# One batch of a sparse-attention and hard-swish kernel goes by four heads with both halves of their queries, and its loads stand between the weights

## The chip, the cores and the metric

One core of one Trainium2 chip. The metric is device time in microseconds (us). Engines are named as the profile names them: PE (TensorE's matmuls; PEld its weight loads), DVE (VectorE), ACT (ScalarE), POOL (GpSimd), SP (SyncE, which here only issues transfers); PEq, SPq and so on are their sequencers.

## What is computed

Attention over 4 batches of 8 heads, 768 positions, 64 features. Each query keeps the 6 chunks of 32 keys with the largest upper bound on its score. The result, laid out as 3072 tokens by 512 features, goes through two dense layers with a hard-swish between them.

```python
ub = np.sum(np.maximum(q[:, :, :, None, :] * k_min[:, :, None, :, :], q[:, :, :, None, :] * k_max[:, :, None, :, :]), axis=-1)
ub = np.where(causal, ub, -1000000000.0)
top_chunks = np.argsort(ub, axis=-1)[..., -top_k:]
scores = scale * np.matmul(q, k.transpose(0, 1, 3, 2))
mask = sel & (pos[:, None] >= pos[None, :])
...
h = x @ w_in
relu6 = np.clip(h + 3.0, 0.0, 6.0)
g = h * relu6 / 6.0
return (g @ w_out).astype(np.float32)
```

## The kernel before

Heads go in 16 pairs; batch b has pairs 4b to 4b+3. Two pairs are a quad (four heads, loaded together). The 768 queries of a head go in two halves of 384. A **unit** is one quad with one half, so a batch has four units, 16 in all. Names of tiles, which are also the names in the rows:

- A unit is prepared (`prepare`): K and Q come from memory (`KS`, `QS`), are transposed (`KF`, `QF`; on DVE for batches 1 to 3), K's chunks give maximum and minimum (`KMA`, DVE's reduces, `limits`), and POOL or ACT casts them to the score operands (`KL`, `QLA`); `QR` is the rectified query.
- `bounds` computes the upper bounds on PE into `UBT`. From batch 1 on, the units are taken two at a time, each on its own corners of the array. In half 0 of batches 1 to 3 only the later 192 queries need full precision: `coarse` units do the first 192 in bf16 (the "guard" matmuls, with `QLA`) and the rest in fp32.
- `attend` picks the chunks on DVE (`UB`, `T`, `SELA`, `MT`), copies the mask beside the query operand (`masks_out`), and then for each pair does the score tiles on PE (`SPS`, two buffers), the exponentials on ACT (`PT`), the causal triangle on POOL, and the product with the values on PE (`PVP`, from `VB`, which POOL casts from `VT`). DVE scales the product into `Xb`. A pair has two score tiles in half 0 (1024 and 512 columns) and four in half 1 (1024, 1024, 768, 1024).
- When the four pairs of a half of a batch are done, its 384 tokens are a group: they are transposed into `XT` (by PE in batch 0, by a transposing transfer from batch 1 on), 16 `hidden` steps of four matmuls give `HP`, ACT or DVE and then DVE turn it into `GT`, and `result` steps of four matmuls each add up `OP` with `WOUT`; ACT or DVE scales that into `OT`, and SP stores it. `WIN` and `WOUT` are each loaded in two halves from POOL's queue, with a cast to bf16. A small copy of a loaded element (`seenWIN`, `seenWOUT`) makes POOL wait for an earlier load before it issues one. The first half of `WOUT` serves result parts 0 and 1, the second half parts 2 and 3.

What stands where is decided by hand-kept tables. `SEQ` gives the order of the first loads (K, Q or V with the number of the unit whose quad is loaded; I and O for halves of `WIN` and `WOUT`); SP has at most three transfers of later batches under way (`ring=3`). `FIRST_TO_LAST` gives the order of all steps on each engine, by step number; every engine then runs its list strictly in that order, waiting where an operand is not there. `LANDED` and the lengths in `add(...)` only feed the program that hands out buffers in that order. PE starts with up to 16 matmuls on zeros (`busy`, line 343 after the change) that do no work of the reference.

Of the kernel before, what the change touches and what calls it, by code (L numbers as in the profile page):

```python
# [135 lines left out]
def kernel(  # L136
# [101 lines left out]

    units = []
    for b in range(B):  # L240
        for half in range(2):
            for n in range(2):
                first = (2 * b + n) * 2
                units.append((pairs[first:first + 2], half))
# [158 lines left out]
    def coarse(b, half):  # L403

        return b > 0 and half == 0
# [11 lines left out]
    def bounds(us):  # L417
# [3 lines left out]
        rough = coarse(us[0]["two"][0]["b"], us[0]["half"])  # L421
        for part, which in ([("guard", 1), ("guard", 0)] if rough else []) + [("all", 1), ("all", 0)]:
            for u in us:
                for i, st in enumerate(u["two"]):
# [242 lines left out]
    SEQ = "K0 Q0 K1 Q1 Q2 K2 V0 V1 Q3 K3 V3 I0 V2 I1 O0 O1 K4 Q4 K5 Q5 V4 V5"  # L667
# [5 lines left out]
    add = plan.add  # L673
# [12 lines left out]
    def arrive(engine, issue, length, run, after=(), take=(), parts=1, ring=False):  # L686
# [3 lines left out]
        for part in range(parts):  # L690
# [5 lines left out]
            if at:  # L696
                behind = [w for w in weights[-1:]] if engine == "POOL" else []
                landed.append(add("WIRE", at, 0, after=[got] + behind, give=lane, least=1.5 if engine == "SP" else 5.6 if behind else 8.8))
                if engine == "POOL":
                    weights.append(landed[-1])  # L700
            else:
                landed.append(add("DMA", length, 0, after=[got], give=lane))
        return landed

    LANDED = dict(SP=[7.05, 7.65, 8.27, 8.87, 9.46, 10.07, 10.67, 11.26, 11.87, 12.47, 13.08, 13.68, 14.28, 14.88, 15.48, 16.08, 16.70, 18.50, 18.95, 19.60, 20.05, 20.45, 20.85, 21.30, 22.30, 22.70, 23.25, 23.80, 26.05, 26.40, 27.30, 41.60, 50.30, 51.40, 52.90, 54.20, 55.70, 57.20, 58.60, 60.00, 61.40, 62.80, 64.10, 64.80, 67.20, 68.80, 69.50, 70.40, 71.40, 72.20, 73.00, 73.70],
                  POOL=[32.30, 37.90, 43.30, 50.10])
# [77 lines left out]
    def prepare(n):  # L784
# [64 lines left out]
        if us:  # L849
# [3 lines left out]
            a = add("PE", 1.25 if len(us) == 1 else 0.8 if coarse(two[0]["b"], half) else 1.27, r + RANK["sel"] + BOUND[n], later(bounds, us), tile=2, after=sum([u["chain"] for u in us], []),  # L853
# [88 lines left out]
    for n_group, ((b, half), xs) in enumerate(finished.items()):  # L942
# [16 lines left out]
        if (b, half) in CROSS:  # L959
            lane = hold("lane")  # L960
            got = add("SP", 1.25, -3000, later(cross_tokens, g), after=xs, take=[held_xt, lane])
            xt.append(add("DMA", 2.0, 0, after=[got], give=[x, x, lane]))
# [11 lines left out]
        for t in range(HB):  # L974
# [21 lines left out]
        PE="""  # L996
# [14 lines left out]
            1574 1569 1575 1576 1570 1577 1581 1585""",  # L1011
        ACT="""
# [81 lines left out]
```

## Time and profile before

| | |
|---|---|
| three timed runs | 265.73 us median (265.18 to 266.31) |
| the profiled execution | 266.49 us |
| its span, first to last instruction | 264.8 us |
| busy PE / DVE / ACT / POOL | 255.5 / 207.7 / 187.2 / 121.6 us |
| moved by transfers | 32.15 MB, mean 121 GB/s |

The span is 1.7 us shorter than the execution's own time, and that execution is 0.76 us above the median of the timed runs. A busy share is an average over stages; matmuls overlap, and their ends are modelled, so a PE that is busy for a whole stretch can still have lost time in it.

### The profile page before, as it was taken

The numbers are of one execution on the slowest core, as the hardware profiler recorded it, in microseconds if no ns is written. First come the engines' busy times: TensorE is split into PE (matmuls) and PEld (weight loads), VectorE is DVE, ScalarE is ACT, GpSimd is POOL, SyncE is SP. The second block draws the span as 40 slices with busy tenths as digits, with TensorE's granted clock in tenths as the row PEclk, the third lists the DMA queues.
The fourth block names the chain that finished last, engine by engine and source line by source line (L and its number), as shares of the span: only waits on it lengthen the run. The fifth ranks groups of instructions, "written<-read, shape, count | busy, mean of one in ns | idle before, by whom it ended". The sixth has DMA issues, their size and how long they took to land.

```text
span 264.8 us, 6528 instructions
## 1 busy us (share of the span) xinstructions
PE 255.5 (96%) x2399; PEld 150.6 (57%) x2424; DVE 207.7 (78%) x577; ACT 187.2 (71%) x308; POOL 121.6 (46%) x282
## 2 busy tenths in 40 slices
PE   6999999999999989999999999999999999999995
PEld 3557566645454666654656575654666666555443
DVE  7889789899897998899877869997986266979001
ACT  3889879667668899847888988855897683634121
POOL 8332834246459775184777382485287221000000
PEclk9999999999999999999999999999999999999999
DMA  8999999999945989997998299832100421301023
GB/s 162 217 201 176 202 202 217 170 128 172 214 97 128 168 158 172 132 146 181 127 132 109 45 185 171 171 62 79 42 1 0 63 79 42 59 4 40 0 82 119
DMA packets 128528, 32.15 MB, mean 121 GB/s; under 512 B 122224, under 2 KB 124528, under 8 KB 128496
## 3 DMA queue, kind: packets, MB, share of 16 engines
q1 hardware_dynamic: 123760, 27.14, 62.9%
q0 software_dynamic: 3136, 4.19, 9.3%
q10 hardware_dynamic: 1600, 0.39, 0.7%
q8 instruction: 19, 0.31, 0.5%
q14 instruction: 13, 0.11, 0.2%
HBM read 27.26 MB, written 6.29 MB: 127 GB/s over the span
## 4 chain that ended last, share of the span: by engine, by line
PE 79%; ACT 6%; DMA 5%; DVE 4%; SPq 2%; issue 2%; ACTq 0%; DVEq 0%
PE OP L631 27%; PE HP L613 27%; PE SPS L517 10%; PE PVP L551 7%; DMA QS<-in_q_dram 5%; ACT PT L529 4%; PE UBT L435 4%; DVE GT L624 2%; PE OP L640 1%; PE SPS L498 1%; SPq L203 1%; ACT U L621 1%; PE SPS L501 1%; DVE QF L359 1%; SPq L195 1%
## 5 line engine op out<-in xcount | busy, mean ns | idle before, releaser
L529 ACT ACTIVATE PT<-SPS 128x1024 bf16<-128x1024 f32 (+2 forms) x96 | 84.8, 915 | 17.3 <-PE SPS L517 12.7
L613 PE MATMUL HP<-XT,WIN 128*128 128x384 bf16 x512 | 91.5, 326 | 0.7 <-DVE GT L624 0.6
L631 PE MATMUL OP<-WOUT,GT 128*128 128x512 bf16 x343 | 85.1, 379 | 1.4 <-issue 0.2
L624 DVE SCALAR_TENSOR_TENSOR GT<-U,HP 128x384 bf16<-128x384 bf16 x128 | 66.2, 544 | 15.0 <-ACT U L621 13.0
L621 ACT ACTIVATE U<-HP,THREE 128x384 bf16<-128x384 f32 x98 | 55.4, 580 | 22.4 <-PE HP L613 19.6
L613 PEld LDWEIGHTS <-WIN 128*128 128x128 bf16 x512 | 48.7, 98 | 33.7 <-issue 1.9
L631 PEld LDWEIGHTS <-GT 128*128 128x128 bf16 x368 | 34.8, 98 | 35.4 <-issue 1.2
L534 POOL TENSOR_SCALAR_AFFINE_SELECT PT<-PT 128x256 bf16<-128x256 bf16 x84 | 33.8, 412 | 38.1 <-ACT PT L529 37.3
L517 PE MATMUL SPS<-QLA,KL 128*128 128x384 bf16 (+2 forms) x240 | 37.8, 278 | 0.9 <-ACT PT L529 0.9
L517 PEld LDWEIGHTS <-KL 128*128 128x128 bf16 x240 | 22.0, 98 | 17.0 <-issue 2.5
L309 POOL TENSOR_SCALAR_AFFINE_SELECT QLA<-QF 64x384 bf16<-64x384 f32 (+1 forms) x43 | 21.4, 502 | 14.3 <-DVE QF L359 11.1
L551 PEld LDWEIGHTS <-PT 128*128 128x128 bf16 x672 | 24.0, 97 | 4.0 <-issue 1.6
L551 PE MATMUL PVP<-VB,PT 128*128 128x65 bf16 x672 | 26.0, 193 | 0.2
L309 POOL TENSOR_SCALAR_AFFINE_SELECT KL<-KF 64x384 bf16<-64x384 f32 x33 | 16.4, 501 | 12.2 <-DVE KF L359 11.2
L619 DVE TENSOR_SCALAR U<-HP 128x384 bf16<-128x384 f32 x30 | 16.5, 551 | 4.5 <-PE HP L613 4.2
L657 ACT ACTIVATE OT<-OP 128x512 f32<-128x512 f32 x15 | 8.9, 592 | 14.5 <-PE OP L631 13.8
L567 DVE TENSOR_TENSOR Xb<-PVP,RINV 128x384 bf16<-128x384 f32 x32 | 17.8, 557 | 1.1
L223 POOL TENSOR_SCALAR_AFFINE_SELECT QLA<-MT 64x768 bf16<-64x768 bf16 x13 | 11.0, 846 | 13.2 <-DVE MT L470 6.9
L359 DVE STREAM_TRANSPOSE KF<-KS 128x384 f32<-128x384 f32 x24 | 13.2, 562 | 1.5 <-DMA KS<-in_k_dram 1.0
L392 ACT ACTIVATE QR<-QF 128x192 bf16<-128x192 f32 (+2 forms) x36 | 12.9, 407 | 1.8 <-DVE QF L359 1.6
L359 DVE STREAM_TRANSPOSE QF<-QS 128x384 f32<-128x384 f32 x24 | 12.5, 548 | 1.9 <-DMA QS<-in_q_dram 1.5
L374 DVE TENSOR_REDUCE KMA<-KF 128x12 f32<-128x384 f32 x24 | 12.9, 539 | 0.2
(89 smaller groups left out, 267.7 us busy)
## 6 DMA issues: line engine op xcount, KB each, us to landing
out_dram<-OT SPq DMA_DIRECT2D x23, 256.0 KB, 2.3
KS<-in_k_dram SPq DMA_DIRECT2D x24, 192.0 KB, 5.2
QS<-in_q_dram SPq DMA_DIRECT2D x24, 192.0 KB, 5.7
VT<-in_v_dram SPq DMA_DIRECT2D x24, 192.0 KB, 4.4
WIN<-in_moe_w_in_dram POOLq DMA_DIRECT2D x2, 1024.0 KB, 9.9
WOUT<-in_moe_w_out_dram POOLq DMA_DIRECT2D x2, 1024.0 KB, 15.2
VS<-in_v_dram SPq DMA_DIRECT2D x12, 128.0 KB, 3.9
KS<-in_k_dram SPq DMA_DIRECT2D x9, 128.0 KB, 3.9
```

What stands on the lines that cost most here:

```text
L309: nc.gpsimd.affine_select(out=to, in_=x, pattern=[[0, n]], compare_op=A.is_ge, fill=0.0, base=0, channel_multiplier=0)
L359: nc.vector.transpose(T[:], st[name][:, st["i"], half * HC:(half + 1) * HC, :].rearrange("p c e -> p (c e)"))
L517: nc.tensor.matmul(SP[:, j, c0:c0 + n], lhsT=KLS[st["pair"] % 6][:, j, jb * P:(jb + 1) * P], rhs=st["QL", half][:, j, at:at + n], start=Tr ...
L529: nc.scalar.activation(PT[:, :, 0:cols], SP[:, :, 0:cols], ACT.Exp, scale=scale)
L534: nc.gpsimd.affine_select(out=PT[:, :, c0:c0 + P], in_=PT[:, :, c0:c0 + P], pattern=[[0, 2], [1, P]], compare_op=A.is_ge, fill=0.0, base=0 ...
L551: nc.tensor.matmul(PVP[:, j, n, :], lhsT=PT[:, j, c0:c0 + P], rhs=st["VB"][:, jb, j, :], start=(jb == 0), stop=(jb == qb))
L567: nc.vector.tensor_tensor(out=to, in0=PVP[:, :, :, 0:D], in1=RINV[:].to_broadcast([P, 2, HB, D]), op=A.mult)
L613: nc.tensor.matmul(HP[:], lhsT=WIN[:, kt, f * P:(f + 1) * P], rhs=g["XT"][:, :, kt, :] if (g["b"], g["half"]) in CROSS else g["XT"][:, kt, ...
L619: nc.vector.tensor_scalar(U[:], g["HP", f][:], 3.0, 0.0, op0=A.add, op1=A.max)
L621: nc.scalar.activation(U[:], g["HP", f][:], ACT.Relu, bias=THREE[:], scale=1.0)
L624: nc.vector.scalar_tensor_tensor(out=g["GT"][:, f, :], in0=g["U", f][:], scalar=6.0, in1=g["HP", f][:], op0=A.min, op1=A.mult)
L631: nc.tensor.matmul(g["OP", t][:], lhsT=g["GT"][:, f, t * P:(t + 1) * P], rhs=WOUT[:, f, :], start=(f == 0), stop=(f == FT - 1))
```

## The change

Units 4 to 7 (batch 1) are numbered anew: before, they were quad 0 half 0, quad 1 half 0, quad 0 half 1, quad 1 half 1; now quad 0 half 0, quad 0 half 1, quad 1 half 0, quad 1 half 1. So the two units that `bounds` takes together are now a coarse and a full one, and the order of its parts goes per unit. In `SEQ` the loads of batch 1's first quad (K4 Q4 V4) stand between the halves of `WIN` and those of `WOUT`, and those of its second quad (now K6 Q6 V6) behind `WOUT`. All five lists of `FIRST_TO_LAST` are new (their numbers are left out here).

```diff
+    BY_QUADS = [1]
     units = []
     for b in range(B):
-        for half in range(2):
-            for n in range(2):
-                first = (2 * b + n) * 2
-                units.append((pairs[first:first + 2], half))
+        for i in range(4):
+            n, half = (i // 2, i % 2) if b in BY_QUADS else (i % 2, i // 2)
+            first = (2 * b + n) * 2
+            units.append((pairs[first:first + 2], half))
...
-        rough = coarse(us[0]["two"][0]["b"], us[0]["half"])
-        for part, which in ([("guard", 1), ("guard", 0)] if rough else []) + [("all", 1), ("all", 0)]:
+        for part, which in (("guard", 1), ("guard", 0), ("all", 1), ("all", 0)):
             for u in us:
+                rough = coarse(u["two"][0]["b"], u["half"])
+                if part == "guard" and not rough:
+                    continue
...
-    SEQ = "K0 Q0 K1 Q1 Q2 K2 V0 V1 Q3 K3 V3 I0 V2 I1 O0 O1 K4 Q4 K5 Q5 V4 V5"
+    SEQ = "K0 Q0 K1 Q1 Q2 K2 V0 V1 Q3 K3 V3 I0 V2 I1 K4 Q4 V4 O0 O1 K6 Q6 V6"
...
-                landed.append(add("WIRE", at, 0, after=[got] + behind, give=lane, least=1.5 if engine == "SP" else 5.6 if behind else 8.8))
+                landed.append(add("WIRE", at, 0, after=[got] + behind, give=lane, least=1.5 if engine == "SP" else 5.6 if behind else 7.9))
...
-                  POOL=[32.30, 37.90, 43.30, 50.10])
+                  POOL=[32.20, 38.40, 57.50, 63.20])
...
     FIRST_TO_LAST = dict(
         PE="""
-            0 1 2 3 4 5 6 148 156 149 157 7 8 9 10 11 12 165 173 164 166 13 174 231 223 14 181 188 230 222 15 190 195 197 238 193 208 248
+            0 1 2 3 4 148 156 149 157 5 6 7 173 165 164 166 174 8 9 10 223 231 11 12 13 14 15 222 181 230 188 190 195 238 197 208 240 193
...
```

How the change moves instructions, at three places. First POOL's queue where `WOUT` is loaded; before, right behind the second half of `WIN`, with the small copy waiting for a V load (`VS`) of batch 0:

```order
L290 COPY seenWIN_634<-VS 1x1
L293 DMA WIN<-in_moe_w_in_dram 128x4x1024
L378 TENSOR_TENSOR KMA<-KMA 128x12 x2
L290 COPY seenWOUT_663<-VS 1x1
L296 DMA WOUT<-in_moe_w_out_dram 128x8x512
```

The same after the change, from the last work ahead of `WOUT` to the casts of V behind its second half:

```order
L291 COPY seenWOUT_1100<-QS 1x1
L297 DMA WOUT<-in_moe_w_out_dram 128x8x512
L310 AFFINE_SELECT KL_107<-KF 64x384
L223 AFFINE_SELECT KL_101<-EB 64x768
L310 AFFINE_SELECT KL_107<-KF 64x384
L310 AFFINE_SELECT QLA<-QF 64x384 x2
L291 COPY seenWOUT_1177<-QS 1x1
L297 DMA WOUT<-in_moe_w_out_dram 128x8x512
```

The load of `WOUT` now waits for the last Q transfer of batch 1's first quad, and four casts of that quad stand between its halves. Second, PE at batch 1's first two `UBT` groups; before, the end of the coarse group and, later, the whole of the full one:

```order
L435 LDWEIGHTS KMA
L435 MATMUL UBT<-QR,KMA 32x192
L435 MATMUL UBT<-QF,KMA 32x192 x8
L435 MATMUL UBT<-QR,KMA 32x192 x8
L631 LDWEIGHTS GT
...
L435 MATMUL UBT<-QF,KMA 32x384 x8
L435 MATMUL UBT<-QR,KMA 32x384 x8
```

After the change, the end of the first group; the second one reads the same:

```order
L438 LDWEIGHTS KMA
L438 MATMUL UBT<-QR,KMA 32x192
L438 MATMUL UBT<-QF,KMA 32x192 x4
L438 MATMUL UBT<-QF,KMA 32x384 x4
L438 MATMUL UBT<-QR,KMA 32x192 x4
L438 MATMUL UBT<-QR,KMA 32x384 x4
L634 LDWEIGHTS GT
```

A group of eight 192-column matmuls and one of eight 384-column ones have become two of four and four. Third, ACT's list from the last exponentials of half 0 in batch 1 (before) to the first `U` of its first group of tokens:

```order
L529 ACTIVATE PT<-SPS 128x2x256
L529 ACTIVATE PT<-SPS 128x1024 x2
L529 ACTIVATE PT<-SPS 128x2x384
L529 ACTIVATE PT<-SPS 128x1024 x3
L529 ACTIVATE PT<-SPS 128x2x384
L529 ACTIVATE PT<-SPS 128x1024 x3
L305 CAST KL_106<-KF 64x384
L529 ACTIVATE PT<-SPS 128x2x384
L529 ACTIVATE PT<-SPS 128x1024
L621 ACTIVATE U<-HP,THREE 128x384 x2
```

The same after the change, for the second quad (pairs 6 and 7), whose half 0 and half 1 now stand together, up to the same `U`:

```order
L532 ACTIVATE PT<-SPS 128x1024
L532 ACTIVATE PT<-SPS 128x2x256
L660 ACTIVATE OT<-OP 128x512
L532 ACTIVATE PT<-SPS 128x1024
L532 ACTIVATE PT<-SPS 128x2x256
L532 ACTIVATE PT<-SPS 128x1024 x2
L532 ACTIVATE PT<-SPS 128x2x384
L532 ACTIVATE PT<-SPS 128x1024 x3
L532 ACTIVATE PT<-SPS 128x2x384
L532 ACTIVATE PT<-SPS 128x1024
L624 ACTIVATE U<-HP,THREE 128x384 x9
```

The exponentials of the first quad (pairs 4 and 5), with casts and copies between them, now stand ahead of these.

## Rows read from the trace of the kernel before

**Rows 1.** The page's line of busy time: us, share of the span, instructions.

```profile
PE 255.5 (96%) x2399; PEld 150.6 (57%) x2424; DVE 207.7 (78%) x577; ACT 187.2 (71%) x308; POOL 121.6 (46%) x282
```

**Rows 2.** Stretches: us, busy PE, PEld, DVE, ACT, POOL (instructions), granted clock, transfers, GB/s.

```profile
90.00:100.00 10.00, 9.10 (x127) 6.41 (x127) 9.61 (x25) 9.66 (x13) 6.23 (x16) 1.00 1.01 178
120.00:260.00 140.00, 138.94 (x1214) 81.69 (x1230) 101.82 (x280) 93.05 (x149) 55.93 (x125) 1.00 0.46 80
```

**Rows 3.** What PE waited for: us in total, times, longest.

```profile
PE SPS L517 <- ACT PT L529: 0.9, 3, 0.4
PE HP L613 <- DVE GT L624: 0.6, 1, 0.6
```

**Rows 4.** Timeline of PE, then DVE, at batch 1's first bounds: start, us, instruction.

```profile
71.77 0.26 PE L435 MATMUL UBT<-QLA,KMA 64*32 64x192 bf16 x4
72.33 0.51 PE L435 MATMUL UBT<-QLA,KMA 64*32 64x192 bf16 x4 [0.29 <-DVE GT L624]
...
73.62 1.67 PE L631 MATMUL OP<-WOUT,GT 128*128 128x512 bf16 x6
...
70.24 1.04 DVE L359 STREAM_TRANSPOSE QF<-QS 128x384 f32<-128x384 f32 x2 [1.28 <-DMA QS<-in_q_dram]
```

**Rows 5.** The chain that ended last: start, us, what (a transfer: issue to landing).

```profile
17.71 1.42 PE UBT L435 x16
...
63.96 6.16 DMA QS<-in_q_dram
...
81.78 1.45 PE UBT L435 x32
...
120.48 0.94 PE UBT L435 x48
...
161.88 6.50 PE HP L613 x40
```

**Rows 6.** Timeline of PE at batch 1's scores: one of three tiles that waited.

```profile
95.91 0.61 PE L517 MATMUL SPS<-QLA,KL 128*128 128x384 bf16 x4 [0.39 <-ACT PT L529]
```

**Rows 7.** The chain in a narrower stretch: a score tile and a values product that waited for nothing.

```profile
88.68 0.44 PE SPS L517 x4
...
93.69 0.92 PE PVP L551 x30
```

**Rows 8.** ACT's exponentials by form: count, busy us, mean ns, idle before.

```profile
L529 ACT ACTIVATE PT<-SPS 128x1024 bf16<-128x1024 f32 x64 | 63.9, 1022 | 11.2 <-PE SPS L517 8.0 <-PE SPS L501 1.5 <-PE SPS L505 1.1
...
L529 ACT ACTIVATE PT<-SPS 128x768 bf16<-128x768 f32 x16 | 12.9, 807 | 4.2 <-PE SPS L517 3.1 <-PE SPS L501 0.9
...
L529 ACT ACTIVATE PT<-SPS 128x512 bf16<-128x512 f32 x16 | 9.6, 599 | 1.9 <-PE SPS L517 1.7
```

**Rows 9.** Transfers: SP's issues (start, us), then `WIN` and `WOUT` by line (ns; starts).

```profile
22.40 19.67 SPq L203 DMA_DIRECT2D KS<-in_k_dram  x4
...
54.31 5.28 SPq L203 DMA_DIRECT2D KS<-in_k_dram  x4
...
L293 POOL DMA_DIRECT2D WIN<-in_moe_w_in_dram x2: 768/880/991, 23.7 to 27.3; - x2
...
DMA to landing us min/median/max: 8.5/9.9/11.4
...
L296 POOL DMA_DIRECT2D WOUT<-in_moe_w_out_dram x2: 891/910/930, 28.5 to 35.5; - x2
...
DMA to landing us min/median/max: 14.9/15.2/15.5
```

**Rows 10.** Timeline of PE at its first results, and at its start.

```profile
49.45 1.02 PE L631 MATMUL OP<-WOUT,GT 128*128 128x512 bf16 x3
...
1.06 3.17 PE L342 MATMUL SPS<-ZERO 128*128 128x512 bf16 x7 [1.06 <-DVE ZERO L251]
...
7.01 1.46 PE L342 MATMUL SPS<-ZERO 128*128 128x512 bf16 x6
```

**Rows 11.** The tile `XT`: its transposing transfers.

```profile
DMA to landing us min/median/max: 3.6/3.8/4.1
```

More of the change, by code (lines that the diff above doesn't have):

```diff
@@ L703, in arrive @@
         return landed
-    LANDED = dict(SP=[7.05, 7.65, 8.27, 8.87, 9.46, 10.07, 10.67, 11.26, 11.87, 12.47, 13.08, 13.68, 14.28, 14.88, 15.48, 16.08, 16.70, 18.50, 18.95, 19.60, 20.05, 20.45, 20.85, 21.30, 22.30, 22.70, 23.25, 23.80, 26.05, 26.40, 27.30, 41.60, 50.30, 51.40, 52.90, 54.20, 55.70, 57.20, 58.60, 60.00, 61.40, 62.80, 64.10, 64.80, 67.20, 68.80, 69.50, 70.40, 71.40, 72.20, 73.00, 73.70],
-                  POOL=[32.30, 37.90, 43.30, 50.10])
+    LANDED = dict(SP=[7.05, 7.65, 8.27, 8.87, 9.46, 10.07, 10.67, 11.26, 11.87, 12.47, 13.08, 13.68, 14.28, 14.88, 15.48, 16.08, 16.70, 18.00, 19.00, 19.60, 20.05, 20.45, 20.85, 21.30, 22.30, 22.80, 23.35, 23.90, 26.00, 26.40, 27.20, 40.00, 41.40, 42.80, 44.20, 45.60, 47.00, 48.40, 49.30, 50.10, 51.00, 51.80, 63.50, 64.90, 66.30, 67.70, 69.10, 70.50, 71.90, 73.30, 74.20, 75.00, 75.90, 76.70],
+                  POOL=[32.20, 38.40, 57.50, 63.20])
     FIRST = dict(KS=(3.65, 4.63), QS=(5.6, 6.43))
@@ L852, in prepare @@
             held = [hold("m") for u in us]
-            a = add("PE", 1.25 if len(us) == 1 else 0.8 if coarse(two[0]["b"], half) else 1.27, r + RANK["sel"] + BOUND[n], later(bounds, us), tile=2, after=sum([u["chain"] for u in us], []),
+            a = add("PE", 1.25 if len(us) == 1 else 0.8 if coarse(two[0]["b"], half) else 1.37 if two[0]["b"] in BY_QUADS else 1.27, r + RANK["sel"] + BOUND[n], later(bounds, us), tile=2, after=sum([u["chain"] for u in us], []),
                     take=held, give=used)
@@ L960 @@
             lane = hold("lane")
-            got = add("SP", 1.25, -3000, later(cross_tokens, g), after=xs, take=[held_xt, lane])
-            xt.append(add("DMA", 2.0, 0, after=[got], give=[x, x, lane]))
+            got = add("SP", 1.42, -3000, later(cross_tokens, g), after=xs, take=[held_xt, lane])
+            xt.append(add("DMA", 1.6, 0, after=[got], give=[x, x, lane]))
         for a in range(0, 0 if (b, half) in WORDS + CROSS else KT_HID, 2):
@@ L996 @@
         PE="""
[14 rows of a table removed]
-            1574 1569 1575 1576 1570 1577 1581 1585""",
-        ACT="""
[10 rows of a table removed]
-            1553 1556 1562 1514 1565 1507 1571 1582 1586""",
-        DVE="""
[13 rows of a table removed]
-            1559 1563 1560 1566 1578""",
-        POOL="""
[8 rows of a table removed]
-            1000 1007 1010 1013""",
-        SP="""
[4 rows of a table removed]
-            1508 1572 1579 1583 1587""",
[14 rows of a table added]
+            1575 1569 1576 1570 1577 1581 1585""",
+        ACT="""
[10 rows of a table added]
+            1494 1523 1526 1529 1535 1538 1541 1544 1547 1550 1556 1559 1562 1507 1500 1565 1514 1571 1582 1586""",
+        DVE="""
[12 rows of a table added]
+            1483 1486 1489 1492 1521 1495 1524 1527 1530 1532 1533 1536 1539 1542 1545 1548 1551 1553 1554 1557 1560 1563 1566 1578""",
+        POOL="""
[7 rows of a table added]
+            878 891 877 953 892 921 881 955 948 899 895 956 896 906 909 988 989 905 961 964 967 974 980 977 997 994 1000 1007 1010 1013""",
+        SP="""
[4 rows of a table added]
+            1572 1579 1583 1587""",
     )
```

94 rows, old and new, of tables (ACT, DVE, PE, POOL) are left out of this document.

## The prediction

> **What bounds the kernel now.** I read the busy line first: PE is busy 255.5 of 264.8 us, and no other engine is over 78% [rows 1]. The stretches say where PE still loses time: from 120 to 260 us it is busy 138.9 of 140, and nothing can be won there, while from 90 to 100 us it is busy 9.1 of 10, with ACT and DVE at 9.7 and 9.6 [rows 2]. So the change can win at most the few waits that PE has ahead of 120 us. The list of PE's waits [rows 3] and the timeline name them, and the reader is to see three. At batch 1's first bounds DVE stands 1.28 us for the last Q transfer, and the `UBT` group behind it takes from 71.77 to 73.62 us, 1.85 us, where the same group at 120.48 takes 0.94 [rows 4, 5]. At batch 1's scores three tiles wait for an exponential to free one of the two score buffers, 0.9 us together, and each then shows 0.60 where an unhindered one shows 0.44 [rows 3, 6, 7]. Once PE waits 0.6 us for a `GT` [rows 3]. All three lie where the order and the loads are new.
>
> **The change, part by part.** The number of score, value, hidden and result matmuls stays. What moves is when they stand, and one group of matmuls changes its form.
>
> *The late Q transfer.* The first bounds of batch 1 now need only the first quad, whose loads stand ahead of `WOUT`. The second half of `WIN` lands at 27.3 + 11.4 = 38.7 us [rows 9]. Then some 6.5 of the quad's eight K and Q transfers are left, at 5.28/4 = 1.32 us each [rows 9]: 47.3 us. PE comes to these bounds at about 63 us (below). POOL's casts for them are queued behind copies that wait for the first half of `WOUT`, at 56 us by the next part, with some eleven instructions, at 0.5 each (an estimate, as DVE's): 61.5. So the wait goes: 1.85 - 0.94 = **-0.9**. The second quad's Q land some seven transfers behind `WOUT`, 62.8 + 9.2 = 72.0; DVE then has about eleven instructions of 0.5 us [rows 4], so the second bounds can begin at some 78, and PE reaches them at 80. That is covered by 2 us; later by more, and it costs PE us for us.
>
> *The exponentials.* Before, from the end of pair 4's last tile to the start of pair 6's last one PE has seven score tiles (five of 0.44 and two of 0.33), one short and two long value products (12 and 30 matmuls, 0.37 and 0.92): 5.1 us, the shorter tiles and products in proportion to the rows [rows 7]. ACT has six exponentials of 1.02 and one of 0.81: 6.9 [rows 8]. The difference is 1.8, the trace shows 0.9 + 3 x 0.16 = 1.35, so ACT's pace is about 0.07 shorter than the means. After, the first quad's exponentials stand between result steps, and the narrow place is the second quad: from the end of pair 6's first tile to the start of pair 7's last one PE has ten score tiles (3.7), three short and three long value products (3.9) and three result steps (2.6): 10.2 us. ACT has seven of 0.95, one of 0.74, two of 0.53 and one scaling of `OT` (0.6, as an exponential of its 512 columns): 9.0. ACT keeps up with 1.2 us to spare: **-1.35**.
>
> *The wait for GT.* It stands behind DVE's reduces. They now stand two at a time between the `GT` instructions. I take **-0.4** (0, if it comes back, to -0.6).
>
> *The bounds in their new form.* Before, two coarse units together take 0.94 and two full ones 1.45, 2.39 in all [rows 5]. After there are two mixed groups. From below: a mixed group holds a full unit, so it is not under 1.42; with 1.45 each it is +0.5. From above: nothing overlaps, 1.42 + 0.94 each, 4.7 in all, +2.3. The nearest row is that a full unit alone takes 1.42 and two take 1.45: the second rides along. The coarse unit's fp32 matmuls then ride along too, and only its guard matmuls have no partner: 0.94 less half of 1.45 is 0.2. So 1.65 each: **+0.9**.
>
> *WOUT later.* PE's first result begins at 49.45 [rows 10]. After, 60 more hidden matmuls stand ahead of it, at 6.50/40 = 0.163 us [rows 5], and a group of 12 transposes (0.7, an estimate by their columns): 59.9. The second half of `WOUT` is asked for eight results and four hidden matmuls on, at 62.3. POOL issues the first half when the quad's last Q lands, 47.3; a first half took 8.5 us with other loads beside it, and the next ones landed 5.3 and 6.4 us apart (38.7, 28.5 + 15.5 = 44.0, 35.5 + 14.9 = 50.4) [rows 9]. That is 56.0, and 61.3 to 62.4 for the second. The quad's four V transfers run beside it, which can cost up to 2.6 us more (an estimate: half of a K transfer each, since K's pieces are half as long). I take 62.9: **+0.6** (0 to 2.5). PE stands idle in that time, and behind the first result on PE stand the hidden steps that feed DVE and ACT.
>
> Here a rule speaks against the change. The rows: while the weights moved, SP needed 19.67 us to get four K transfers out, and 5.28 without them [rows 9]; the weights kept their 5.3 to 6.4 us. So it is the K transfers that yield. The Trainium skill, "DMA: Bandwidth & Descriptors", section "Queues, rings and completion order", says that each transfer engine goes round-robin between the queues it has work for. The trace agrees only in that both move; the turns are not of equal worth here. With turns of equal worth the three K transfers under way would hold up `WOUT` by their whole length, which is the slower rival below.
>
> *Tokens of batch 1's half 0.* They are complete only after pair 7, and from that product to the first hidden step PE has 5.1 us (six score tiles, two long products, one result step). The transfer takes 3.6 to 4.1 [rows 11], which leaves 1.0 for DVE's two scaling instructions. **+0.2** (0 to 0.7, one more DVE instruction ahead).
>
> *Start and stores.* PE now has five fillers ahead of the first transposes instead of seven; it waits for K and Q there anyway: 0 (-0.3 to +1.1, a rival). Stores move on SP, but nothing waits for them.
>
> Sum: -0.9 - 1.35 - 0.4 + 0.9 + 0.6 + 0.2 = -0.95. The profiled execution took 266.49, so 265.5; it stands 0.76 above the median of the runs, 265.73, so on that scale **264.8 us**.
>
> **Rivals.**
>
> *All covers hold.* `WOUT` and the tokens come in time, and the mixed bounds cost their least: -0.9 - 1.35 - 0.6 + 0.5 = -2.35, so 263.4. For it: 2 to 6 us of margin on the first quad. Against: every new cover is an estimate from a transfer's pace.
>
> *WOUT is held up (slower).* Place: the third result part on PE, at 62.3. The K transfers of the second quad are in the queue beside `WOUT`; if two of the three go ahead in full, 2 x 1.32 later, the second half lands at 65.6 and PE waits 3.3 instead of 0.6: 267.5. It decides from a landing of about 65.2 on, where the time is 0.5% above before. For it: SP's queue will have three transfers ready the moment V is in. Against: how the weights kept their pace before.
>
> *The exponentials are only crowded elsewhere, so the change does not do what it says.* The second quad has both halves at one place. If two result steps of PE fall out of that place by a wait of ACT's casts or mask copies, ACT is 0.5 us short of PE, and with the hand-overs the old 1.35 comes back: 266.1. Against: the 1.2 us to spare.
>
> *The clock at the start.* Seven matmuls of 512 columns take 3.17 us at the start, six take 1.46 from 7.01 [rows 10]: the first run at the lower of the two levels, 1.2 GHz, the later at 2.4, though the granted clock reads 1.00 throughout. Before the rise PE was at work without a gap. With five fillers there is a gap ahead of the first transposes. If the clock rises only some us later, the first bounds (1.42 at the higher level [rows 5]) take 1.4 longer, part of it under the wait for Q: +1.1, 265.9. The Trainium skill, "TensorE: Matmul & The Clock Gate", section "What's actually happening", says that the default state is throttled and that activity releases it; by that, less activity ahead can mean a later rise, and the trace of before cannot show it.
>
> **How the numbers follow.** Forecast 264.8, by its own terms 264.0 to 265.6: 0.46. All covers hold, 263.4: 0.24. `WOUT` held up, 267.5: 0.15. Exponentials crowded, 266.1: 0.08. Clock, 265.9: 0.07. 0.5% of 265.73 is 1.33 us, about what a measurement of this kernel can tell from no change: faster is under 264.4, slower over 267.06. Faster: nearly all of the second case and a third of the first, 0.40. Slower: most of the third, 0.14. The same: 0.46. The range reaches from the best case's lower side to the bound where the slower rival decides: 262.9 to 267.1.
>
> **What would show it.** Right: the first `UBT` group of batch 1 runs at about 63 us without a wait for Q; both take 1.5 to 1.8 us; no score tile of batch 1 waits for an exponential; the first result begins near 60, with a wait under 1 us for `WOUT` two parts on; from 120 us on the trace reads as before. Wrong: a wait of over 2 us of PE at the first results; a wait of DVE for K or Q of the first quad, behind which `GT` stands and so PE's hidden steps; the first hidden step of batch 1 waiting for `XT`; a start in which the transposes of the first Q keep the lower clock.

## The result, and the profile after

The changed kernel takes 268.74 us (median of six runs, 266.80 to 270.39) beside 265.60 for the kernel before: ratio 1.0122, 95% interval 1.0091 to 1.0154. The forecast was 264.8. The profiled execution took 269.50 (span 267.8), and it stands 0.76 above its median, as the one of before did. Medians here and below are over all runs of a kernel; ratios leave out the runs in which the chip showed its slower state.

PE's part of the line of busy time has grown little (before: [rows 1]); the list of PE's waits says where the rest went. The page's line, then the waits (us in total, times, longest):

```profile
PE 257.2 (96%) x2402; PEld 151.6 (57%) x2424; DVE 204.3 (76%) x571; ACT 194.1 (73%) x320; POOL 119.5 (45%) x276
```

```profile
PE OP L634 <- DMA WOUT<-in_moe_w_out_dram: 2.3, 1, 2.3
PE HP L616 <- ACT PT L532: 1.1, 1, 1.1
...
PE SPS L520 <- ACT PT L532: 0.2, 1, 0.2
```

The last of these lines and the absence of a wait for `GT` answer to [rows 3]: the scores' wait fell from 0.9 to 0.2 us. The other two lines are new. The second is put down to an exponential, but what PE stood for at 32.9 us was the first half of `WIN`: it was issued at 23.0 and landed 11.0 later, at 34.0; PE's weight loads stand 1.4 us for it, and the first hidden step begins at 34.09. The stretches behind 90 us (columns as in [rows 2]) say that the second half of the program is in order:

```profile
90.00:100.00 10.00, 9.75 (x113) 6.41 (x113) 8.67 (x32) 9.36 (x14) 6.00 (x14) 1.00 1.09 212
120.00:260.00 140.00, 139.11 (x1213) 81.66 (x1227) 104.54 (x287) 96.30 (x156) 52.26 (x118) 1.00 0.41 76
```

The loss is at the first results. The timeline of PE there, and one line of DVE:

```profile
61.77 1.89 PE L634 MATMUL OP<-WOUT,GT 128*128 128x512 bf16 x7
63.49 0.81 PE L616 MATMUL HP<-XT,WIN 128*128 128x384 bf16 x4
66.60 1.59 PE L634 MATMUL OP<-WOUT,GT 128*128 128x512 bf16 x4 [2.29 <-DMA WOUT<-in_moe_w_out_dram]
...
69.98 0.58 DVE L442 STREAM_TRANSPOSE UB<-UBT 128x384 f32<-128x384 f32 x1 [4.42 <-PE UBT L438]
```

The chain that ended last (a transfer: issue to landing) goes through the second half of `WOUT`, which lands at 54.18 + 12.37 = 66.55, and shows both `UBT` groups of batch 1. Ahead of that issue it goes through POOL's casts of Q (`QLA`) and the transpose on DVE that they wait for:

```profile
52.29 0.58 DVE QF L360
52.93 0.50 POOL QLA L310
53.49 0.51 POOL QLA L310
54.18 12.37 DMA WOUT<-in_moe_w_out_dram
66.60 1.59 PE OP L634 x4
68.19 2.52 PE UBT L438 x32
...
86.14 1.48 PE UBT L438 x32
```

The same form of group takes 1.48 us at 86 and 2.52 at 68. One-microsecond stretches say why (the last three columns: granted clock, transfers, GB/s):

```profile
64.00:65.00 1.00, 0.31 (x2) 0.08 (x1) 0.97 (x3) 1.00 (x3) 0.93 (x3) 1.00 1.33 202
65.00:66.00 1.00, 0.00 (x0) 0.00 (x0) 0.55 (x1) 0.38 (x1) 0.19 (x1) 1.00 0.47 72
66.00:67.00 1.00, 0.40 (x2) 0.19 (x2) 0.00 (x0) 0.00 (x0) 0.00 (x0) 0.96 0.83 135
67.00:68.00 1.00, 1.00 (x3) 0.15 (x1) 0.00 (x0) 0.00 (x0) 0.00 (x0) 0.50 1.10 167
68.00:69.00 1.00, 1.00 (x25) 0.74 (x32) 0.00 (x0) 0.00 (x0) 0.00 (x0) 0.50 1.44 148
69.00:70.00 1.00, 1.00 (x24) 0.38 (x9) 0.02 (x1) 0.00 (x0) 0.00 (x0) 0.50 1.64 137
70.00:71.00 1.00, 0.84 (x9) 0.21 (x3) 0.78 (x2) 0.00 (x0) 0.28 (x1) 0.84 1.52 134
```

PE stands still from 64.3 to 66.6 us. DVE, ACT and POOL finish what they have and are empty from 66 on, because all that they could do next comes from PE, whose list has the waiting result in front. From 67 to 70 us the granted clock is 0.50, the lower of the two levels (1.2 GHz). So in this execution PE pays twice: 2.3 us of waiting, and then more for the same work. What it costs at the higher level (2.4 GHz) the chain of e1, below, shows, where PE hardly waited:

```profile
64.59 1.02 PE OP L634 x4
65.61 1.48 PE UBT L438 x32
```

Beside these the four result matmuls took 0.57 us more in the changed kernel and the bounds 1.04: 1.6 us together.

### The profile page after: what moved, and what is told of

It reads as the page before. It is cut to its first block, busy times and chain, and to the rows that moved or that the text cites. A ratio compares the mean times of both kernels' runs of the same rounds, so it can differ in the third digit from the quotient of the medians.

```text
span 267.8 us, 6526 instructions
## 1 busy us (share of the span) xinstructions
PE 257.2 (96%) x2402; PEld 151.6 (57%) x2424; DVE 204.3 (76%) x571; ACT 194.1 (73%) x320; POOL 119.5 (45%) x276
## 3 DMA queue, kind: packets, MB, share of 16 engines
q1 hardware_dynamic: 123760, 27.14, 62.9%
## 4 chain that ended last, share of the span: by engine, by line
PE 86%; DMA 6%; ACT 2%; DVE 2%; issue 2%; POOL 0%; ACTq 0%; DVEq 0%
PE OP L634 29%; PE HP L616 26%; PE SPS L520 10%; PE PVP L554 7%; PE UBT L438 5%; DMA WOUT<-in_moe_w_out_dram 5%; PE SPS L501 2%; ACT PT L532 2%; PE QT L351 2%; PE SPS L504 2%; DMA QS<-in_q_dram 1%; PE OP L643 1%; PE SPS L343 1%; PE KT L351 1%; DVE GT L627 1%
## 5 line engine op out<-in xcount | busy, mean ns | idle before, releaser
L627 DVE SCALAR_TENSOR_TENSOR GT<-U,HP 128x384 bf16<-128x384 bf16 x128 | 67.7, 547 | 19.7 <-ACT U L624 16.8
L624 ACT ACTIVATE U<-HP,THREE 128x384 bf16<-128x384 f32 x100 | 57.0, 581 | 27.0 <-PE HP L616 20.7
L660 ACT ACTIVATE OT<-OP 128x512 f32<-128x512 f32 x18 | 10.7, 595 | 19.2 <-PE OP L634 19.2
L310 POOL TENSOR_SCALAR_AFFINE_SELECT KL<-KF 64x384 bf16<-64x384 f32 x36 | 18.1, 506 | 5.2 <-DVE KF L360 3.9
L310 POOL TENSOR_SCALAR_AFFINE_SELECT QLA<-QF 64x384 bf16<-64x384 f32 (+1 forms) x34 | 16.9, 502 | 6.0 <-DVE QF L360 4.5
L622 DVE TENSOR_SCALAR U<-HP 128x384 bf16<-128x384 f32 x28 | 15.5, 553 | 3.4 <-PE HP L616 3.3
L223 POOL TENSOR_SCALAR_AFFINE_SELECT QLA<-MT 64x768 bf16<-64x768 bf16 x14 | 11.6, 830 | 11.0 <-DVE MT L473 10.6
L442 DVE STREAM_TRANSPOSE UB<-UBT 128x384 f32<-128x384 f32 x16 | 9.0, 572 | 9.3 <-PE UBT L438 9.2
L393 ACT ACTIVATE QR<-QF 128x384 f32<-128x384 f32 (+2 forms) x36 | 12.6, 408 | 2.0 <-DVE QF L360 1.9
## 6 DMA issues: line engine op xcount, KB each, us to landing
WIN<-in_moe_w_in_dram POOLq DMA_DIRECT2D x2, 1024.0 KB, 10.9
```

The lines of the kernel that those rows point to most:

```text
L310: nc.gpsimd.affine_select(out=to, in_=x, pattern=[[0, n]], compare_op=A.is_ge, fill=0.0, base=0, channel_multiplier=0)
L622: nc.vector.tensor_scalar(U[:], g["HP", f][:], 3.0, 0.0, op0=A.add, op1=A.max)
L624: nc.scalar.activation(U[:], g["HP", f][:], ACT.Relu, bias=THREE[:], scale=1.0)
L627: nc.vector.scalar_tensor_tensor(out=g["GT"][:, f, :], in0=g["U", f][:], scalar=6.0, in1=g["HP", f][:], op0=A.min, op1=A.mult)
```

## Experiments

The kernel before had 265.6 to 266.1 us beside all of them. The two times of `WOUT` are read from the one profiled execution of each run. In e3, e4 and e14 that execution is 1.5 to 1.8 us faster than the median, in e2 and e5 1.0 to 2.0 slower, so these times and the median belong together only roughly. The theory: the second half of `WOUT` lands late because its load is issued late, PE has nothing else in front, and the clock falls behind the wait. Rivals: transfers beside `WOUT` hold it up; the start is what is late.

| run | edit | first half of `WOUT` issued, second half landed | median us | ratio, 95% interval |
|---|---|---|---|---|
| changed kernel | | 49.4, 66.6 | 268.74 | 1.0122 [1.0091, 1.0154] |
| e1 | first half of `WOUT` behind K | 41.5, 64.5 | 266.88 | 1.0055 [1.0032, 1.0077] |
| e2 | second quad's loads behind `WOUT` | 49.1, 64.7 | 272.09 | 1.0242 [1.0184, 1.0299] |
| e3 | matmuls on zeros in the wait | 48.8, 65.2 | 268.31 | 1.0081 [1.0053, 1.0109] |
| e4 | seven fillers at the start | 48.5, 64.8 | 268.09 | 1.0084 [1.0044, 1.0123] |
| e5 | both halves of `WOUT` behind K | 41.2, 57.9 | 272.51 | 1.0208 [1.0167, 1.0249] |
| e6 | halves of `WIN` close together | 48.9, 65.9 | 269.05 | 1.0089 [1.0055, 1.0123] |
| e7 | before, with five fillers | | 265.68 | 0.9990 [0.9970, 1.0011] |
| e8 | e4 + e5 + e6 | 42.5, 59.4 | 272.41 | 1.0225 [1.0192, 1.0257] |
| e9 | first half behind the third Q | 45.0, 64.0 | 267.23 | 1.0061 [1.0034, 1.0088] |
| e10 | bounds ahead of the waiting result | 49.2, 66.6 | 266.59 | 1.0038 [1.0020, 1.0056] |
| e11 | e9 + e10 | 45.2, 63.5 | 266.16 | 1.0014 [0.9993, 1.0034] |
| e12 | e11 + e4 | 46.1, 66.1 | 266.09 | 1.0016 [0.9997, 1.0035] |
| e13 | e11, `WIN` behind a K transfer | 47.6, 66.7 | 267.13 | 1.0061 [1.0033, 1.0090] |
| e14 | e13 + e4 | 46.6, 65.7 | 267.96 | 1.0078 [1.0043, 1.0113] |

**e1, the first half of `WOUT` earlier.** On POOL's list its issue moves up past five triangles and two mask copies, and it waits for K's last part:

```diff
+            if what == "O0":
+                held_back, last = last, keys4
             there[name, n] = arrive("POOL", 0.95, 6.4, (load_weights, name, n, last[1]), after=last[0])
...
-            298 304 301 326 315 312 318 330 108 352
+            298 108 304 301 326 315 312 318 330 352
```

> Only the place of the first half of WOUT changes: POOL issues it when batch 1's K transfers of the first quad are in (about 42 us) and no longer when its Q are in (49.4). Theory A (WOUT lands late because no load of weights was under way from 40.5 to 49.4, when transfers moved 132 to 171 GB/s instead of some 210): the idle room is used, second half lands near 63.5 instead of 66.6, PE's wait of 2.3 us and the fall of the granted clock behind it go: 264.5 to 265.3 us. Rival B (the late landing comes from K6 and V4 beside it and these only move along): second half at 65.5 or later, wait of 1.5 us and more, 267 to 268.5. Rival C (Q of the first quad becomes late instead, and the first bounds of batch 1 wait for it as before the change): no wait for WOUT, but a wait at the first UBT group of 1 us or more, 266 to 267.

The second half landed at 64.5, a microsecond later than said, and PE waited 0.2 us for it. The time fell by 1.9 us, but not to 265. So an earlier landing makes the kernel faster, and rival B falls as to the wait. The reason that was given did not hold: from 40 to 50 us the transfers moved 157 GB/s and not 210 (152 in the changed kernel), so the earlier load did not fill the room that was thought idle. The loads traded places: the last Q came at 52.4 instead of 48.2, and the first hidden steps waited 0.5 us for a `GT` (rival C, in small and at another place). The chain shows where the late Q went:

```profile
41.16 11.22 DMA QS<-in_q_dram
...
52.50 0.59 DVE QF L360
...
53.15 0.45 POOL QLA L310
...
54.40 10.14 DMA WOUT<-in_moe_w_out_dram
```

POOL issues the second half of `WOUT` behind its casts of Q, and these wait for Q and for DVE. So the second half was issued at 54.40, no earlier than in the changed kernel, although the first half was issued 8 us earlier.

**e2, nothing of the second quad beside `WOUT`.**

```diff
+        if name == "KS" and not part and two[0]["pair"] == 6:
+            nc.sync.dma_start(two[0][name][0:1, 0, 0, 0:1], WOUT[0:1, FT - 1, DMODEL - 2:DMODEL].bitcast(FP32))
```

> SP holds the K, Q and V transfers of batch 1's second quad back until the second half of WOUT has landed (a transfer of four bytes of WOUT into the K tile's place stands ahead of them). WOUT is issued as in the changed kernel, at 49.4 and 54.2. If the three K transfers beside WOUT hold it up (by their bytes, 3 x 0.196 MB at about 0.2 MB per us): second half lands near 63.6, wait gone, 264.7 if the second bounds still find their Q, up to 2 more if not. If WOUT keeps its own pace whatever is beside it, so that only its issue counts: it lands at 65.5 to 66.6 and the time is 268 to 270.

A transfer of four bytes of `WOUT` into the K tile stands ahead of the second quad's loads on SP and makes them wait. From the first half's issue to the second's landing it took 53.85 + 10.9 - 49.11 = 15.6 us; in the profiles with the same issue and the transfers beside it, it took 16.2 to 17.4 (changed kernel, e3, e4, e6, e10). So these transfers cost `WOUT` some 0.6 to 1.8 us by single profiles, not the 2.9 of their bytes. Of the 15.6 us, 4.7 pass before POOL issues the second half. The landing, 64.7, lies between the two that were expected, and the time above both. It is longer because K and Q of the second quad now come too late: DVE stands 6.8 us for K, the masks of the first quad stand behind that in its list, and PE waits 4.3 us at the scores. The Trainium skill, "DMA: Bandwidth & Descriptors", section "Queues, rings and completion order", has the transfer engines go round-robin between the queues that have work. If a turn of either queue were worth the same, three K transfers (1.32 each [rows 9]) would cost 4.0 (an estimate). The traces agree that both move, not that they share evenly.

**e3, matmuls on zeros in the wait.**

```diff
+        if (g["b"], g["half"], t, part) == (0, 0, 0, 2):
+            for _ in range(11):
+                nc.tensor.matmul(g["OP", t][:], lhsT=ZERO[:], rhs=..., start=False, stop=False)
```

> Eleven matmuls on zeros (0.22 us each, they add zero to the result) stand where PE waits for the second half of WOUT; nothing else changes and WOUT lands at 66.6 as before. If the fall of the granted clock after the idle time costs (0.50 from 67 to 70 us: the four result matmuls and the UBT group took 1.59 and 2.52 us where full clock gives 0.87 and 1.48): the clock stays at 1.00 there, and the time falls by 1.5 to 1.9 us, to about 267.0. Rival: the stall itself is the whole loss, since DVE and ACT have run dry and the first bounds come at 68 whatever the clock: 268.2 to 268.9.

The granted clock's mean was 0.998 or more in all ten runs; in the changed kernel it was 0.993 or 0.994 in four of six, and these four took 268.6 to 270.4 where the other two took 267.9 and 266.8. So the fillers do keep the clock up, and in the chain of the profile the `UBT` group takes 1.48 us again. But the time fell only by 0.4, to 268.31, which is where the rival had it (the stall alone is the loss), not the theory (267.0). The profile can't settle why. It is one of the two fastest executions of ten (266.47; the others took 267.5 to 268.7), and in it `WOUT` landed at 65.2, while PE began the result at 65.36, straight from the last of the fillers: where `WOUT` lands that early, the fillers themselves hold PE up. Single profiles do show a price. The execution's time less `WOUT`'s landing is 203.0 and 203.3 us where the clock fell (changed kernel, e6), and 201.3 to 202.4 where it did not (e1, e3, e4, e9). What the clock costs in the median is not shown.

**e4 and e7, the start.** The same exchange in the changed kernel (five to seven) and in the one before (seven to five):

```diff
-            0 1 2 3 4 148 156 149 157 5 6 7 173
+            0 1 2 3 4 5 6 148 156 149 157 7 173
```

> Seven matmuls on zeros ahead of the first transposes as before the change, instead of five; the rest is the changed kernel. Both theories of the start say that the first transposes of K take 1.1 us instead of 1.7 and the first bounds of the second unit begin near 12.9 instead of 14.4. If WOUT's landing decides (chain of transfers, not of PE): PE only waits longer for it, 2.3 us become about 3, and the time stays at 268.2 to 269. Rival (the start is on the path): 0.7 us faster, 267.6 to 268.1.

> The kernel before with five matmuls on zeros ahead of the first transposes instead of seven, as in the changed kernel; nothing else. If the gap on PE ahead of the first transposes keeps its clock at the lower level for longer (transposes of K 1.7 us instead of 1.1, first bounds 0.4 and 1.5 us later): 266.2 to 267.2 us. If the start waits for K and Q anyway: within 0.3 of the time before, 265.4 to 266.0.

Neither moved the time beyond the intervals. In e7 the start was indeed late: its first bounds began at 11.06 instead of 9.05, its first hidden step at 33.87 instead of 32.60. Yet its span is 264.0. The timeline of DVE, then PE, at batch 1's first bounds shows two more things:

```profile
69.26 1.00 DVE L359 STREAM_TRANSPOSE QF<-QS 128x384 f32<-128x384 f32 x2
...
72.02 0.28 PE L435 MATMUL UBT<-QLA,KMA 64*32 64x192 bf16 x8
```

DVE does not wait for Q here, where it stood 1.28 us in the profile of before [rows 4]; nor does any line for a wait for `GT` stand in e7's list. The last of the Q transfers was issued at 63.0 and landed 5.8 us later, at 68.8, where in the profile of before it landed at 70.1. So the two waits may be those of one execution, one that stood 0.76 above the median; with one profile of each, the two moved fillers can't be ruled out. What PE had lost at the start was made up by this place, whose bounds waited for nothing.

**e5, both halves early.** As e1, with the second half's issue right behind the first's.

> Both halves of WOUT are issued one behind the other as soon as the first quad's K transfers are in (about 41.5 and 42.5 us); the rest is the changed kernel. If the place of WOUT's issue is the cause: the halves land near 52 and 58, no run waits for them (PE needs the second at 64), the granted clock does not fall, and the time is 265.0 to 266.0, 3 us under the changed kernel: what is left over the time before is the first hidden step's wait for WIN (0.6 to 1.5 us) and the mixed bounds (0.66). Rival (Q of the first quad yields now and comes too late): its last part lands after 60 and the first UBT group of batch 1 waits over 1 us: 266.5 to 268. Rival (what the run with only the first half early has left over, 266.9, has nothing to do with WOUT): 266.5 to 267.2.

`WOUT` landed as forecast, 52.3 and 57.9. The first rival happened, at another place. The timeline of DVE, then PE:

```profile
58.97 1.04 DVE L360 STREAM_TRANSPOSE QF<-QS 128x384 f32<-128x384 f32 x2 [6.82 <-DMA QS<-in_q_dram]
...
60.50 4.00 PE L616 MATMUL HP<-XT,WIN 128*128 128x384 bf16 x12 [6.59 <-DVE GT L627]
```

The last Q, issued at 42.4, lands 16.4 us later. DVE has its transpose in its list ahead of the `GT`s of the first hidden steps, so PE's hidden steps stand 6.6 us. The first bounds, for which Q is loaded, wait for nothing.

**e6 and e8, `WIN`'s halves close together; and three edits at once.**

```diff
-            74 246 272 319 265 252 268 322 271 82 279
+            74 82 246 272 319 265 252 268 322 271 279
```

> POOL issues the second half of WIN right behind the first (24 to 25 us instead of 29.5), as close as before the change; the rest is the changed kernel. Theory (the weights get more of the transfer engines when POOL's queue holds two of them): the first half lands at 32.2 as before and not at 33.2 to 34.1, PE's wait at the first hidden step falls from 0.5 to 1.4 us to under 0.3, and the K and Q transfers of the first quad come later by what WIN gains, so WOUT, which waits for them, lands at 66 or later and the time stays at 268.2 to 269.5. Rival (only the sum of bytes counts): first half at 33 to 34 and PE's wait as in the changed kernel.

> The changed kernel with three edits: both halves of WOUT behind the first quad's K, the second half of WIN right behind the first, seven matmuls on zeros ahead of the first transposes. If the account is right (a kernel without WOUT's wait and without WIN's takes what the run with matmuls on zeros took less those matmuls, 264.1 to 264.5): 263.8 to 265.0 us, faster than both. Rival (loads only trade places: Q of the first quad is late now): 266 or more, with a wait at the first UBT group of batch 1.

In e6 the first half of `WIN` landed at 33.5, inside the 33 to 34 of the rival, so the theory about two loads in POOL's queue falls; the time is that of the changed kernel. e8 has e5's wait (5.9 us for `GT`) and nothing to show beside it.

**e9 to e11, the two remedies.** e9 lets the first half of `WOUT` wait for Q's third part, not its fourth; e10 changes PE's list alone; e11 has both.

```diff
+            if what == "O0":
+                seen = last[0][:3], lambda: units[4][0][0]["QS"][64:65, 1, NCH - 1, 31:32]
...
-            1068 1069 1135 1070 368 1071
+            1068 1069 1135 368 1070 1071
```

> The first half of WOUT waits for the third of the first quad's four Q transfers and no longer for the fourth, and stands ahead of three triangles and a mask copy on POOL: issued near 45.7 us instead of 48.5 to 49.4. In the profiles so far the second half lands 16.2 to 17.1 us after the first one's issue, and the time is 201.8 us behind that landing where the granted clock does not fall (202.9 to 203.2 where it does). So it lands at 62.3 to 62.8, ahead of PE (63.1 to 64.2): no wait, and the time is that of PE's path, 264.3 to 265.5. Rival (the last Q yields to WOUT by more than 3 us, so that DVE, which has it in its list ahead of GT, holds up the hidden steps): a wait of PE for GT of 1 us or more, 266 to 268.

> On PE alone the first bounds of batch 1 change places with the third result part, the first that needs the second half of WOUT; their operands are ready at 64.1 us in the changed kernel. WOUT lands as late as there (64.8 to 66.6). If the loss is that PE's list has nothing else ahead of the late half: the 1.5 us of bounds fill the wait, DVE and ACT get the bounds at 65.7 instead of 70, the granted clock stays at 1.00, and the time is 201.8 - 1.5 us behind the landing: 265.5 to 266.9. Rival (the first bounds are themselves ready only as late as WOUT, or the banks that they take hold up PE): no gain, 268 to 269.

> Both edits: the first half of WOUT behind the third Q transfer, and the bounds ahead of the third result part. If the two are right PE's result needs the second half 1.5 us later and it lands 3 us earlier, so no run waits for it: 264.0 to 265.3 us, with less spread than either. Rival (Q late on DVE's list): as in the kernel with the first edit alone, 266 to 268.

In e10 `WOUT` landed as late as in the changed kernel, 66.6. Its timeline of PE:

```profile
63.28 0.81 PE L616 MATMUL HP<-XT,WIN 128*128 128x384 bf16 x4
64.02 0.26 PE L438 MATMUL UBT<-QLA,KMA 64*32 64x192 bf16 x4
...
65.01 0.82 PE L438 MATMUL UBT<-QR,KMA 64*32 64x384 f32 x8
66.63 2.75 PE L634 MATMUL OP<-WOUT,GT 128*128 128x512 bf16 x12 [0.80 <-DMA WOUT<-in_moe_w_out_dram]
```

In e9 POOL issued the first half of `WOUT` at 45.0 (45.7 was said), and PE waited for no `GT`, but the second half landed at 64.0, a microsecond and a half later than said: PE waited 0.6 us, and the time was missed by 1.7. The expectation had tied that landing to the first half's issue. But the second half was issued at 53.37, only 0.8 earlier than in the changed kernel, since it stands behind the same casts of Q, for which POOL stood 1.7 us idle. No run moves the issue of the second half alone; that is the remedy left untried. In e10 the bounds fill the wait, 0.8 us of it are left, the granted clock was 0.999 or more in all twelve runs, and the time fell by 2.15 us with the transfers untouched. That is the plainest proof of the cause: the same late landing costs 2 us less when something else stands in front. It does not part the wait from the clock, since both are smaller. In e11 `WOUT` lands at 63.5 and PE waits for it not at all; its stretch beside the one of the changed kernel (from 60 to 70 us):

```profile
60.00:70.00 10.00, 10.00 (x84) 4.78 (x83) 9.55 (x37) 7.02 (x17) 5.04 (x14) 1.00 1.43 164
```

```profile
60.00:70.00 10.00, 7.65 (x63) 3.69 (x66) 5.54 (x13) 5.36 (x13) 4.09 (x11) 0.85 1.23 169
```

At 266.16 it is level with the kernel before, 0.9 us over the range that was expected.

**e12 to e14, what is left.** e11 with seven fillers; with `WIN`'s first half behind batch 0's last K transfer; with both.

```diff
+            if what == "I0":
+                seen = keys3
```

> The last kernel (first half of WOUT behind the third Q transfer, bounds ahead of the third result part) with seven matmuls on zeros ahead of the first transposes instead of five. Where a late load held PE up later on, a late start cost nothing (the kernel before with five: no change). With that wait gone, what PE loses at the start should now count: the first hidden step comes at 32.6 to 33.2 instead of 33.5, and the time is 0.3 to 0.8 us under the 266.2 of the last kernel: 265.3 to 265.9. Rival (PE at the start waits for K, Q and WIN whatever it does ahead of them): 266.0 to 266.4.

> The last kernel with the first half of WIN issued behind batch 0's last K transfer and no longer behind a V transfer, some 2 us earlier (21.2 us). If WIN's landing (33.2 to 33.8 us) holds up the first hidden step: it lands near 31.5, PE gains 0.3 to 0.8 us, 265.4 to 265.9. Rival (PE comes to that step at 33.5 by itself after the late start): 266.0 to 266.4; and if the V transfers that WIN passes come late, the first value products wait and it is slower.

> Both. If start and WIN bound the first hidden step in turn, only this one gains in full: first hidden step at 32.0 to 32.6 us, 264.8 to 265.5 us, at or under the time before. If neither binds: 266.0 to 266.4.

None gained. In e12 the first hidden step came at 32.56 as forecast, a microsecond earlier than in e11, but `WOUT` landed at 66.1 (0.4 us of waiting behind the bounds), and PE waited 1.1 us for POOL at the values products near 48 us. In e13 `WIN` was issued at 22.65 instead of 23.58, not 21.2, because the K transfer that it waits for landed only at 22.5; now it stood ahead of batch 1's K, the first K part took 10.0 us to land instead of 4.9, and everything behind it moved: last Q, `WOUT` at 66.7. PE did not wait for that `WOUT`, but 1.6 us for POOL at the values products near 49 us. That wait, 1.3 us in e14, belongs to e9's edit: POOL stood 3.0 to 3.6 us at the copy that waits for Q, with the triangles of these products behind it. No version beats the kernel before.

## Why the prediction was wrong, point by point

- **`WOUT` later, +0.6: the step that failed.** It said: issued at 47.3, landed at 56.0 and 62.9, PE there at 62.3. Measured: issued at 49.44, landed at 59.84 and 66.55, PE ready at 64.3, so a wait of 2.3 in place of 0.6. PE was 2.0 us late itself, the load 3.65. Of these 3.65, 2.1 lie ahead of the issue. The last Q came at 48.2 (41.7 + 6.5), 0.9 late, but POOL reached the copy that waits for it only at 49.31, behind a triangle and a mask copy (0.82). So POOL's own list set the issue, and the prediction had not timed it. Another 1.7 lie in the first half's way: 10.4 us instead of 8.7. The 8.5 behind that figure is one transfer of one execution [rows 9]; in no run of the new order did the first half of `WOUT` take less than 9.8. The interval between the halves came out (6.7 for 6.9), but not as said: the second half's issue, 54.18, hung on the casts of Q in POOL's list. From 40.5, when `WIN` is in, to 49.4 no weights were under way, and it is tempting to see the cause there. From 40 to 50 us the first line is the changed kernel, the second the kernel before, the third e1:

```profile
40.00:50.00 10.00, 9.87 (x132) 6.30 (x131) 8.94 (x20) 8.94 (x14) 4.69 (x10) 1.00 1.05 152
```

```profile
40.00:50.00 10.00, 9.89 (x124) 6.28 (x124) 9.41 (x20) 8.73 (x12) 3.83 (x8) 1.00 1.43 211
```

```profile
40.00:50.00 10.00, 9.87 (x133) 6.33 (x131) 9.13 (x21) 8.88 (x14) 6.38 (x12) 1.00 1.18 157
```

  With the first half of `WOUT` under way from 41.5 the total is 157 GB/s and not 211: weights at work there do not bring the old rate back, so their absence is not shown to be what made `WOUT` late. Its own slower rival (65.6, wait 3.3, 267.5; chance 0.15) named the right wait with the wrong main reason: e2 gives K beside `WOUT` 0.6 to 1.8 us.
- **The clock behind a wait: a term that was missing.** 0.57 + 1.04 = 1.6 us in the trace of one execution; its share of the median is not shown (e3). The prediction had the clock only at the start, as a rival. There it did not matter (e4, e7).
- **The first hidden step** waited 1.1 us for `WIN`, which the prediction had not looked at; e13 showed that it can't be had earlier for nothing. In the other profiles of the new order the wait is 0 to 0.9 us, and why the first half of `WIN` took 11.0 us here and 8.7 to 10.8 there stays open.
- Together: 265.5 (forecast on the scale of the profiled execution) + (2.3 - 0.6) + 1.6 + 1.1 - 0.3 (bounds, next point) = 269.6; the profiled execution took 269.5. That it closes proves little: it is one profile, the terms overlap (a late hidden step also delays the issue of `WOUT`), and in e7 the first hidden step began at 33.87 and the time was not longer.
- **The mixed bounds, +0.9:** 1.48 each at full clock, 2 x 1.48 - 2.39 = +0.57. The second unit rides along even better than said.
- **The exponentials, -1.35:** right as to the mechanism; the size was not measured by itself. The wait fell from 0.9 to 0.2 us, and from 90 to 100 us PE is busy 9.75 instead of 9.10 of 10. e7's profile of the old order has the 0.9 again, so this gain is not one execution's.
- **Late Q -0.9, `GT` -0.4:** both waits are gone, but e7 suggests that they were those of the one profiled execution. The prediction took them off that execution and then took off 0.76 more for its place above the median: the same time twice, if e7's one profile speaks for the others. It would explain most of why e11, without the waits for `WOUT` and `WIN`, stands at 266.2 and not at 264.8. That is argued, not shown: no further profile of the old kernel was made. The late first hidden step of e11 (33.54 instead of 32.60) is not shown to be the rest: e12 began it at 32.56 and gained nothing. One more wait of PE stands in every profile of the new order and in neither of the old: 0.7 us at a score tile of batch 0, near 17 us. No run tried it.
- **Tokens, +0.2:** no wait for `XT` is listed in the changed kernel, 0.2 to 0.6 us in most of the other runs (0.6 in e1, 0.3 in e11). Right.
- **Second bounds:** no wait at 86.14, as said; how much margin was left is not shown.

What stays open is the last half microsecond between e11 and the kernel before, which is within its interval.

## What to carry to other kernels

When a load is moved, follow its issue through the list of the engine that issues it. Here the second half of `WOUT` stood behind casts that wait for another engine, so that issuing the first half 8 us earlier (e1) brought the second half's issue no earlier. And ask who pays for an earlier load: the last Q came 4 us later in e1 and 10.6 later in e5. Where an engine has to stand for a load, put work that is ready in front of it (2.15 us here, from one exchange in a list). And do not subtract a wait that one profile shows and, besides, that profile's distance from the median.

## What was not expected of the hardware

- The granted clock fell to 0.50 behind a wait of PE of 2.3 us (2.2 in e6), and stayed at 1.00 in the profiles with a wait of 1.4 (e4) or 0.8 (e10). The Trainium skill, "TensorE: Matmul & The Clock Gate", section "What's actually happening", says that the throttled state is the default and activity lifts it; by that the fall belongs to the idle time, and the trace agrees: no fall with fillers in the wait (e3). The mean clock was lower in four of the six executions of the changed kernel and not in the other two.
- With the granted clock read as 1.00, six transposes of the first K took 1.38 to 1.89 us with five fillers ahead and 1.13 to 1.74 with seven, from one execution to the next; the time did not follow the fillers (e4, e7).
- The order of issue went with large differences: the same K part took 4.9 us to land when issued ahead of `WIN` (e11) and 10.0 just behind it (e13), and a Q part behind two halves of `WOUT` took 16.4 (e5).
- Weights beside the small pieces of SP's queue did not add to the total: from 40 to 50 us 152 GB/s moved without them (changed kernel) and 157 with them (e1, e5), although the kernel before had 211 there.
